# One sum and one reciprocal for a pair of heads, queries and keys in token order, and shorter preparations, in an attention and expert kernel

## The chip, the cores and the metric

The kernel runs on one core of a Trainium2 chip. The core has a matrix engine (TensorE, PE in the profile, with its weight loads shown as PEld), a vector engine (VectorE, DVE), an activation engine (ScalarE, ACT), GpSimd (POOL) and SyncE (SP), which issues nearly all DMAs here. Each engine works through its own queue of instructions in order and waits on semaphores of the others. The metric is the time of one execution in microseconds (us) on the device; the times shown are medians of several executions.

## The reference

Three layers follow each other, on 4 sequences of 576 tokens with width 512 (8 heads of 64):

```python
scores = scale * np.matmul(q, k.transpose(0, 1, 3, 2))
cum = np.cumsum(np.maximum(s, 0.0), axis=-1)
bias = -(cum[:, :, :, None] - cum[:, :, None, :])
scores = np.where(causal, -1000000000.0, scores + np.minimum(bias, 0.0))
attn = np.exp(scores - np.max(scores, axis=-1, keepdims=True))
attn = attn / (np.sum(attn, axis=-1, keepdims=True) + 1e-09)
x = np.matmul(attn, v)                      # attention, heads side by side
h = gelu(x @ w_in); u, v = halves of h      # gated layer
x = x + (u * (w_sg @ layernorm(v) + b_sg)) @ w_out
e = argmax of x @ w_gate, or the token before's choice if sigmoid(x @ w_local) >= 0.5
out = p[e] * (relu(x @ w1[e]) @ w2[e])      # one of 8 experts per token
```

## The kernel before

The attention of all 32 heads runs first, in pairs of heads, mixed with the gated layer of the sequences that are complete; the experts come last. The program is written in Python generators that interleave the stages, and a scheduler then orders the instructions of each engine by its own estimate of when each is ready. A change of one instruction can therefore move others on every engine.

Values are kept as a high part of reduced precision (fp32r) and a low part that is the rest, so that three products stand for one fp32 product.

**Queries and keys.** `prep_load(p)` fetches q and k of a pair of heads into the tiles `nq` and `nk`: 96 partitions, each with 6 neighbouring tokens of both heads (`"h (p r) d -> p r h d"`, one DMA per tile). `prep_T(p, c)` handles half `c`: three transposes on TensorE (L344) put 96 tokens each side by side into a PSUM bank; ACT writes the high part into the tile `qk` (L353 for q, L356 for k), DVE the low part (L354, L357). Since partition p held the tokens 6p to 6p+5, a transpose r gives every sixth token, and the four copies write (and DVE reads) every sixth element of the row: `x.rearrange("p (t r) -> p r t", r=6)`.

**The first four pairs** (sequence 0) are row-tiled: the two heads of a pair lie on partitions 0 to 63 and 64 to 127, and `emit_R(p, i)` computes 128 queries of both. The later pairs go head by head through `emit_S`. For each, DVE adds the causal mask and takes the row minimum (L411), `soft` then has ACT compute the exponential and the row sum (L417), POOL add 1e-9 (L418), DVE take the reciprocal (L419) and POOL scale the rows (L420); L502 transposes the result, DVE and ACT copy it into `et` (L508, L506 for heads 0 to 7), and L541 multiplies it with v. The last 64 queries of both heads are done together (`emit_tail`, L841).

**The sums of s.** `emit_first` makes the running sums for the heads of sequence 0 (eight broadcast DMAs, clamp L223, scan L224, and on to `cumr` at L233), which the first row minimum needs through one matmul. `emit_cum` makes them for all 32 heads, 32 rows on as many partitions: clamp (L239), scan (L241), five subtractions of the value at the start of each block of 128 queries (L246), two copies of the high part (L247), two subtractions for the low part (L248) and two DMAs to a table `cum_d` in memory, out of which later heads fetch their rows. It stands behind the row minimum that was written last when it is reached, in pair 2.

**Constants.** `emit_consts2` builds small tables for the routing to experts: POOL makes them, and some thirteen short DVE instructions convert them (L309 to L330). They have no order with respect to the rest.

The weights of the gated layer come in between as 8-byte numbers and are converted by L723 (ACT), L724 and L727 (DVE), L728 (POOL), L729 (ACT) and L730 (DVE).

## Time and profile before

| | |
|---|---|
| time, median of 3 runs | 843.71 us (842.79 to 845.37) |
| the profiled execution's own time | 844.22 us |
| its span | 842.4 us |
| granted TensorE clock, mean over the span | 0.978 |
| busy: TensorE, weight loads, DVE, ACT, POOL | 792.2, 678.2, 532.1, 449.9, 349.1 us |
| DMA: moved, mean rate | 133.33 MB, 158 GB/s |

The profile is of one execution. Busy times are shares of the span in which the engine had an instruction at work; TensorE's matmuls overlap, and their ends are modelled. The rows further on come from views in order of time (start, duration, engine, line, operation, tiles, and in brackets how long the engine stood idle before and what ended this), from groups of like instructions (busy time, mean of one in ns, idle time before), and from tables of stretches.

### The profile page before, as it was taken

Reading aid. Unit: us, or ns where it says so; the run is one execution under the profiler, and the core shown is the slowest. Engines: PE = TensorE matmul, PEld = TensorE weight load, DVE = VectorE, ACT = ScalarE, POOL = GpSimd, SP = SyncE. Lnnn points to the kernel's source line nnn. Section 1 sums busy time; section 2 is a strip of 40 time slices with the busy share of each in tenths; the row PEclk is TensorE's granted clock in tenths of the full one; section 3 lists DMA queues with packets and bytes.
Section 4 is the critical chain, followed back from the end, with each engine's and each line's share of the span. In section 5 each row is a group of like instructions: output and inputs, shape, how many; then the busy total and the mean of one; then the engine's idle time right before and its main releaser. Section 6 shows DMA issues by size and latency. Waiting matters only on the chain. (4 is left out here: it accounts for less than half of the span.)

```text
span 842.4 us, 14677 instructions
## 1 busy us (share of the span) xinstructions
PE 792.2 (94%) x4828; PEld 678.2 (80%) x4828; DVE 532.1 (63%) x1489; ACT 449.9 (53%) x1040; POOL 349.1 (41%) x627
## 2 busy tenths in 40 slices
PE   8797998989999999999998999989999999999995
PEld 4564687779879889878788788778989989899894
DVE  7777577876768788867786476774555444353420
ACT  5676577766637786527784245134454344443510
POOL 5785556576434387614586001052022222313101
PEclk9699999999999999999999999999999999999998
DMA  8565699794488587587450763144564544535300
GB/s 186 137 184 142 153 229 306 192 237 99 93 192 231 153 214 174 130 238 201 92 179 18 255 220 123 51 139 142 178 211 122 176 127 146 186 126 184 125 5 35
DMA packets 117735, 133.33 MB, mean 158 GB/s; under 512 B 69184, under 2 KB 82624, under 8 KB 117656
## 3 DMA queue, kind: packets, MB, share of 16 engines
q1 hardware_dynamic: 113816, 122.87, 53.6%
q0 software_dynamic: 3840, 9.48, 3.0%
q8 instruction: 40, 0.66, 0.3%
q14 instruction: 39, 0.32, 0.1%
HBM read 91.07 MB, written 23.13 MB: 136 GB/s over the span
## 5 line engine op out<-in xcount | busy, mean ns | idle before, releaser
L1211 DVE TENSOR_TENSOR wp<-wraw,wp 128x1024 fp32r<-128x1024 f32 x63 | 76.6, 1223 | 96.6 <-ACT wp L1210 96.0
L841 PE MATMUL ps<-wp,hT 128*128 128x512 f32 x528 | 123.0, 392 | 0.0
L1267 POOL DMA_INDIRECT out_dram<-y,ids x24 | 34.9, 1454 | 204.6 <-ACT y L1266 157.0
L841 PE MATMUL ps<-xT,wp 128*128 128x384 f32 x672 | 119.1, 336 | 0.0
L841 PEld LDWEIGHTS ps<-xT,wp 128*128 128x128 f32 x672 | 117.3, 188 | 0.7
L841 PEld LDWEIGHTS ps<-wp,hT 128*128 128x128 f32 x528 | 98.6, 188 | 21.1
L1210 ACT CAST wp<-wraw 128x1024 fp32r<-128x1024 f32 x64 | 66.5, 1050 | 65.3 <-DMA wraw<-in_moe_w_dram 58.6
L417 ACT ACTIVATE E<-E,negm 128x128 f32<-128x128 f32 (+4 forms) x136 | 79.1, 582 | 35.5 <-DVE negm L411 30.5
L420 POOL TENSOR_SCALAR E<-E,lsum 128x128 f32<-128x128 f32 (+4 forms) x136 | 79.6, 588 | 38.1 <-DVE lsum L419 28.4
L541 PE MATMUL ps<-et,vv 128*128 128x320 f32 (+9 forms) x476 | 82.7, 314 | 9.9 <-DVE et L508 5.7
L418 POOL TENSOR_SCALAR lsum<-lsum 128x1 f32<-128x1 f32 x144 | 34.5, 240 | 124.7 <-ACT E L417 111.2
L541 PEld LDWEIGHTS ps<-et,vv 128*128 128x128 f32 (+1 forms) x476 | 65.1, 171 | 25.1 <-ACT wsg L247 5.4
L502 PE MATMUL ps<-ident,E 128*128 128x128 f32 (+1 forms) x452 | 69.2, 266 | 8.9 <-POOL E L420 5.5
L411 DVE CUSTOM_DVE_ANT_0 E<-ps,zmask 128x128 f32<-128x128 f32 (+4 forms) x136 | 63.5, 474 | 17.8 <-PE ps L841 15.4
L841 PE MATMUL ps<-wsg,vg 128*128 128x288 f32 x448 | 68.3, 304 | 2.0 <-DVE g L850 1.0
L510 ACT CAST et<-ps 128x384 fp32r<-128x384 f32 (+3 forms) x120 | 50.6, 431 | 33.4 <-PE ps L502 31.4
L841 PEld LDWEIGHTS ps<-wsg,vg 128*128 128x128 f32 x448 | 62.3, 192 | 3.3 <-DVE g L850 1.2
L502 PEld LDWEIGHTS ps<-ident,E 128*128 128x128 f32 (+1 forms) x452 | 48.0, 142 | 20.6 <-POOL E L420 6.9
L511 DVE TENSOR_TENSOR et<-ps,et 128x384 fp32r<-128x384 f32 (+3 forms) x120 | 56.8, 483 | 7.2 <-ACT et L510 6.8
L841 PE MATMUL ps<-xh,w 128*128 128x288 f32 x256 | 57.6, 303 | 0.6 <-DVE negm L411 0.5
L1255 DVE SCALAR_TENSOR_TENSOR hT<-ps,hT 128x384 fp32r<-128x384 f32 x56 | 30.3, 553 | 40.4 <-ACT hT L1254 40.4
L841 PE MATMUL ps<-w,vg 128*128 128x512 f32 (+1 forms) x216 | 54.5, 396 | 0.0
(305 smaller groups left out, 1624.7 us busy)
## 6 DMA issues: line engine op xcount, KB each, us to landing
wraw<-in_moe_w_dram SPq DMA_DIRECT2D x64, 512.0 KB
qk<-qk SPq DMA_DIRECT2D x24, 432.0 KB
w<-wv_d SPq DMA_DIRECT2D x16, 512.0 KB
w<-wo_d SPq DMA_DIRECT2D x16, 512.0 KB
qk<-qk SPq DMA_DIRECT2D x24, 288.0 KB
w<-wu_d SPq DMA_DIRECT2D x12, 512.0 KB
nq<-in_q_dram SPq DMA_DIRECT2D x16, 288.0 KB
nk<-in_k_dram SPq DMA_DIRECT2D x16, 288.0 KB
```

Source lines behind the costliest of these rows:

```text
L411: hred[g] = DVE.tensor_tensor_reduce(out=e[:, a:z], in0=pt[:, 0:z - a], in1=zmask[:, m0:m0 + z - a], scale=-1.0, scalar=BIG if hi == 0 els ...
L417: ACT.activation(out=x, in_=x, func=ACTF.Exp, scale=-1.0, bias=nm, accum_out=l)
L418: POOL.tensor_scalar(out=l, in0=l, scalar1=1e-9, scalar2=0.0, op0=ALU.add, op1=ALU.add)
L420: POOL.tensor_scalar(out=x, in0=x, scalar1=l, scalar2=1.0, op0=ALU.mult, op1=ALU.mult)
L502: PE.transpose(pt[:, j * M:(j + 1) * M], e[h, 128 * j:128 * (j + 1)], ident[h, h])
L510: ACT.copy(out=dst[0], in_=src)
L511: DVE.tensor_tensor(out=dst[1], in0=src, in1=f32v(dst[0]), op=ALU.subtract)
L541: PE.matmul(x, lhsT=l, rhs=rhs if g >= F4 else f32v(rhs), start=(j == 0 and n_ == 0), stop=(j == js[-1] and n_ == len(ms) - 1),)
L841: ms = [PE.matmul(pt, lhsT=l, rhs=r, start=(first_ and x == 0), stop=(last_ and x == n - 1)) for x, (l, r) in enumerate(pairs)]
L1210: c = ACT.copy(out=w[:, 0, :], in_=r)
L1211: a = (POOL if (e, j) == (0, KD) else DVE).tensor_tensor(out=w[:, 1, :], in0=r, in1=f32v(w[:, 0, :]), op=ALU.subtract)
L1267: POOL.indirect_dma_start(out=of[:, :], out_offset=bass.IndirectOffsetOnAxis(ap=idx, axis=0), in_=y, in_offset=None, bounds_check=NT - 1, ...
```

## The change

It consists of five parts.

1. In `soft`, the two heads of a row-tiled pair keep their row sums in two columns of one tile. One addition and one reciprocal serve both columns, after both exponentials.
2. `prep_load` fetches the 576 tokens in two halves of 288, each with 3 neighbouring tokens to a partition: two DMAs per tile with pieces of half the length.
3. `prep_T` places the three transposes of a half so that their columns interleave in the PSUM bank (each writes every third element); the bank then holds 288 tokens in order, and ACT and DVE read and write rows without a step.
4. `emit_cum` handles only the 24 heads of sequences 1 to 3, with one row for each head and block on 120 partitions: five DMAs bring the same rows five times, one clamp and one scan run over all, three short instructions pick the value at each block's start, and one subtraction, one copy, one subtraction and one DMA follow.
5. All DVE instructions of `emit_consts2` are ordered behind the first row minimum of head 1.

```diff
     def emit_cum():
-        R = 128 // NH
-        s_sb = T(mp, [128, S], F32, "u2", bufs=5)[0:NH]
-        dma(s_sb, s.rearrange("b h s -> (b h) s"))
-        behind(DVE.tensor_scalar_max(out=s_sb, in0=s_sb, scalar1=0.0), hred[max(hred)].ins.name)
-        cum = s_sb
-        DVE.tensor_tensor_scan(out=cum, data0=one[0:NH], data1=s_sb, initial=0.0, op0=ALU.mult, op1=ALU.add)
-        for P, i0, z0 in ((128, 0, 6), (NH, R, 8)):
-            tmp = T(mp, [128, S], F32, "u2", bufs=5)
-            ch = wsg[0:P, z0:z0 + 2, :]
-            for a in range(P // NH):
-                DVE.tensor_scalar(out=tmp[NH * a:NH * a + NH], in0=cum, scalar1=cum[:, 128 * (i0 + a):128 * (i0 + a) + 1], scalar2=None, op0=ALU.subtract)
-            ACT.copy(out=ch[:, 0, :], in_=tmp[0:P])
-            DVE.tensor_tensor(out=ch[:, 1, :], in0=tmp[0:P], in1=f32v(ch[:, 0, :]), op=ALU.subtract)
-            dma(cum_d[:, NH * i0:NH * i0 + P, :].rearrange("z p s -> p z s"), ch)
+        n = NH - H
+        P = NQ * n
+        rows, cum = [T(mp, [128, S], F32, "u2", bufs=5)[0:P] for _ in range(2)]
+        src = s.rearrange("b h s -> (b h) s")[H:NH]
+        for i in range(NQ):
+            dma(rows[n * i:n * i + n], src)
+        behind(DVE.tensor_scalar_max(out=rows, in0=rows, scalar1=0.0), hred[max(hred)].ins.name)
+        DVE.tensor_tensor_scan(out=cum, data0=one[0:P], data1=rows, initial=0.0, op0=ALU.mult, op1=ALU.add)
+        m = T(mp, [128, NQ], F32, "m5")[0:P]
+        ref = T(mp, [128, 1], F32, "mr")[0:P]
+        DVE.tensor_reduce(out=m, in_=ident[0:P, 0:P].rearrange("p (i c) -> p i c", c=n), axis=AX.X, op=ALU.add)
+        DVE.tensor_tensor(out=m, in0=cum.rearrange("p (i c) -> p i c", c=64)[:, 0::2, 0], in1=m, op=ALU.mult)
+        DVE.tensor_reduce(out=ref, in_=m, axis=AX.X, op=ALU.add)
+        DVE.tensor_scalar(out=rows, in0=cum, scalar1=ref, scalar2=None, op0=ALU.subtract)
+        ch = wsg[0:P, 6:8, :]
+        ACT.copy(out=ch[:, 0, :], in_=rows)
+        DVE.tensor_tensor(out=ch[:, 1, :], in0=rows, in1=f32v(ch[:, 0, :]), op=ALU.subtract)
+        dma(cum_d.rearrange("z p s -> p z s"), ch)
...
         for src, nm in ((q, "nq"), (k, "nk")):
             t = T(ap_, [96, 6, 2, D], F32, nm)
-            dma(t, src[b, h0:h0 + 2].rearrange("h (p r) d -> p r h d", p=96))
+            for a in range(2):
+                dma(t[:, 3 * a:3 * a + 3], src[b, h0:h0 + 2, HS * a:HS * a + HS].rearrange("h (p r) d -> p r h d", p=96))
...
     def emit_consts2():
+        def late_(x):
+            behind(x, hred[1].ins.name)
...
-        DVE.tensor_copy(out=w8d, in_=it[:, 0:8])
+        late_(DVE.tensor_copy(out=w8d, in_=it[:, 0:8]))
...
             for r in range(3):
-                PE.transpose(pt[:, 96 * r:96 * r + 96], n[:, 3 * c + r].rearrange("p h d -> p (h d)"), ident[0:96, 0:96])
-
-            def v6(x):
-                return x.rearrange("p (t r) -> p r t", r=6)[:, 3 * c:3 * c + 3, :]
-
-            src = pt[:, 0:HS].rearrange("p (r t) -> p r t", r=3)
-            hi = v6(t[:, a, :])
-            lo = v6(t[:, 2 + a, :])
+                PE.transpose(
+                    pt[:, 0:HS].rearrange("p (t r) -> p r t", r=3)[:, r], n[:, 3 * c + r].rearrange("p h d -> p (h d)"), ident[0:96, 0:96]
+                )
+            src = pt[:, 0:HS]
+            hi, lo = [t[:, z, HS * c:HS * c + HS] for z in (a, 2 + a)]
...
-    def soft(x, nm, l):
-        ACT.activation(out=x, in_=x, func=ACTF.Exp, scale=-1.0, bias=nm, accum_out=l)
+    def soft(xs, nms, l):
+        for z, (x, nm) in enumerate(zip(xs, nms)):
+            ACT.activation(out=x, in_=x, func=ACTF.Exp, scale=-1.0, bias=nm, accum_out=l[:, z:z + 1])
         POOL.tensor_scalar(out=l, in0=l, scalar1=1e-9, scalar2=0.0, op0=ALU.add, op1=ALU.add)
         DVE.reciprocal(out=l, in_=l)
-        POOL.tensor_scalar(out=x, in0=x, scalar1=l, scalar2=1.0, op0=ALU.mult, op1=ALU.mult)
+        for z, x in enumerate(xs):
+            POOL.tensor_scalar(out=x, in0=x, scalar1=l[:, z:z + 1], scalar2=1.0, op0=ALU.mult, op1=ALU.mult)
...
-        for r in range(2):
-            soft_of(2 * p + r, i, e[r], nm[r])
+        soft_of(2 * p, i, e, nm)
```

The lines of `prep_T` and `row_min` shift by one: L353 to L357 and L411 of before are L352 to L356 and L410 of after.

The order of instructions moves on all engines. On DVE at the start, before (`u` holds the running sums, `ga` the tables that POOL made, `E` the scores and `negm` their minimum):

```order
L357 TENSOR_TENSOR qk_25_97<-ps,qk_25_97 128x3x96
L320 TENSOR_SCALAR first_84<-s_12_83 128x5
L312 CAST io_8_79<-ga_268 128x128
L223 TENSOR_SCALAR u_39_159<-u_39_159 128x576
L354 SCALAR_TENSOR_TENSOR qk_25_97<-ps,qk_25_97 128x3x96
L313 CAST ioc_80<-ga_268 128x144
L357 TENSOR_TENSOR qk_25_97<-ps,qk_25_97 128x3x96
L316 TENSOR_SCALAR ga_268<-ga_268 128x20
L321 TENSOR_SCALAR ltri_86<-io_8_79,pidx_81 128x128
L224 SCALAR_TENSOR_TENSOR u_40_160<-u_38_148,u_39_159 128x576
```

and after:

```order
L353 SCALAR_TENSOR_TENSOR qk_25_97<-ps,qk_25_97 128x288
L356 TENSOR_TENSOR qk_25_97<-ps,qk_25_97 128x288
L353 SCALAR_TENSOR_TENSOR qk_25_97<-ps,qk_25_97 128x288
L356 TENSOR_TENSOR qk_25_97<-ps,qk_25_97 128x288
L223 TENSOR_SCALAR u_39_161<-u_39_161 128x576
L224 SCALAR_TENSOR_TENSOR u_40_162<-u_38_150,u_39_161 128x576
L226 TENSOR_TENSOR cs_193<-u_40_162,e_44_174 128x5
```

All four low parts of the first pair now precede the clamp L223, and the scan L224 follows it at once; the constants stand behind the first two row minima.

On ACT around the sixth weight tile (`vg`, converted by L723), before:

```order
L729 CAST w_99_541<-vg_542 128x512
L723 ACTIVATE g_116_680<-vg_678 128x512
L417 ACTIVATE E_102_578,lsum_484<-E_102_578,negm_580 128x384
L353 ACTIVATE qk_25_97<-ps 128x3x96
L356 CAST qk_25_97<-ps 128x3x96
L553 COPY xf_457<-ps 64x320
```

and after:

```order
L729 CAST w_101_537<-vg_538 128x512
L352 ACTIVATE qk_25_97<-ps 128x288
L355 CAST qk_25_97<-ps 128x288
L417 ACTIVATE E_104_574,lsum_590<-E_104_574,negm_576 128x384
L723 ACTIVATE g_120_676<-vg_674 128x512
L553 COPY xf_457<-ps 64x320
```

L723 has moved behind the two `qk` copies and the exponential.

On DVE around `emit_cum`, before:

```order
L730 TENSOR_TENSOR vg_831<-vg_831 128x512
L411 ISA E_148_946,negm_948<-ps,zmask_73 128x512
L411 ISA negm_948 128x1
L246 TENSOR_SCALAR u_143_894<-u_142_890 32x576 x3
L419 RECIPROCAL lsum_781<-lsum_781 128x1
L246 TENSOR_SCALAR u_143_894<-u_142_890 32x576
L246 TENSOR_SCALAR u_144_902<-u_142_890 32x576
L411 ISA ga_947,negm_949<-ps,zmask_73 128x512
L411 ISA negm_949 128x1
L508 COPY et_425<-ps 128x5x64
L508 COPY et_425<-ps 128x128
```

and after:

```order
L410 ISA E_154_940,negm_942<-ps,zmask_73 128x512
L410 ISA negm_942 128x1
L730 TENSOR_TENSOR vg_823<-vg_823 128x512
L247 TENSOR_TENSOR m_149_890<-u_148_882,m_149_890 120x5
L410 ISA ga_941,negm_943<-ps,zmask_73 128x512
L410 ISA negm_943 128x1
L419 RECIPROCAL lsum_874<-lsum_874 128x2
L508 COPY et_425<-ps 128x5x64
L508 COPY et_425<-ps 128x128
```

The five subtractions of 576 columns no longer stand ahead of the copies L508; one product of 5 columns does.

## Rows read from the trace of the kernel before

**Rows 1.** The page, busy time of each engine.
```profile
PE 792.2 (94%) x4828; PEld 678.2 (80%) x4828; DVE 532.1 (63%) x1489; ACT 449.9 (53%) x1040; POOL 349.1 (41%) x627
```

**Rows 2.** Stretches: length, busy PE, PEld, DVE, ACT, POOL, clock, DMA share, GB/s.
```profile
8.00:37.00 29.00, 23.13 (x126) 14.59 (x124) 27.90 (x85) 18.82 (x49) 19.64 (x40) 0.77 0.74 166
72.00:76.00 4.00, 3.94 (x12) 1.94 (x12) 2.46 (x10) 1.52 (x5) 3.10 (x5) 0.66 0.49 174
76.00:450.00 374.00, 355.64 (x2451) 308.09 (x2452) 282.87 (x916) 250.51 (x670) 214.45 (x449) 0.99 0.70 180
100.00:160.00 60.00, 56.95 (x397) 48.95 (x396) 43.54 (x128) 42.99 (x119) 32.60 (x67) 0.97 0.95 256
```

**Rows 3.** DVE in order of time, 8 to 16 us: start, duration, engine, line.
```profile
7.95 0.67 DVE L357 TENSOR_TENSOR qk<-ps,qk 128x288 fp32r<-128x288 f32 x1 [0.65 <-ACT qk L356]
...
8.74 0.45 DVE L223 TENSOR_SCALAR u<-u 128x576 f32<-128x576 f32 x1
9.11 0.67 DVE L354 SCALAR_TENSOR_TENSOR qk<-ps,qk 128x288 fp32r<-128x288 f32 x1
...
9.82 0.67 DVE L357 TENSOR_TENSOR qk<-ps,qk 128x288 fp32r<-128x288 f32 x1
...
10.63 1.35 DVE L224 TENSOR_TENSOR_SCAN u<-u,u 128x576 f32<-128x576 f32 x1
...
15.58 0.34 DVE L411 CUSTOM_DVE_ANT_0 E<-ps,zmask 128x128 f32<-128x128 f32 x1
```

**Rows 4.** SP's queue in order of time, the first loads.
```profile
0.73 0.76 SPq L78 DMA_DIRECT2D nq<-in_q_dram  x1
...
2.31 4.43 SPq L200 DMA_DIRECT2D u<-in_s_dram  x8
```

**Rows 5.** Groups by line and shape: count, busy us, mean ns, idle before.
```profile
L356 ACT CAST qk<-ps 128x288 fp32r<-128x288 f32 x32 | 24.3, 758 | 0.9 <-PE ps L344 0.9
...
L354 DVE SCALAR_TENSOR_TENSOR qk<-ps,qk 128x288 fp32r<-128x288 f32 x32 | 22.6, 707 | 6.6 <-ACT qk L353 6.3
...
L357 DVE TENSOR_TENSOR qk<-ps,qk 128x288 fp32r<-128x288 f32 x32 | 22.2, 694 | 0.7 <-ACT qk L356 0.7
...
L850 DVE SCALAR_TENSOR_TENSOR u<-ga,ps 128x288 f32<-128x288 f32 x32 | 14.2, 444 | 1.6 <-ACT ga L849 1.4
...
L511 DVE TENSOR_TENSOR et<-ps,et 128x320 fp32r<-128x320 f32 x24 | 11.6, 483 | 3.7 <-ACT et L510 3.4
...
L510 ACT CAST et<-ps 128x320 fp32r<-128x320 f32 x24 | 10.2, 425 | 10.9 <-PE ps L502 9.5 <-PE ps L541 1.1
```

**Rows 6.** Two lines from 8 to 37 us: count, least, median, most ns.
```profile
L354 DVE SCALAR_TENSOR_TENSOR qk<-ps,qk x4: 659/668/684, 9.1 to 32.1; 128x288 fp32r<-128x288 f32 x4
...
L419 DVE RECIPROCAL lsum<-lsum x13: 139/151/215, 17.2 to 34.4; 128x1 f32<-128x1 f32 x13
```

**Rows 7.** ACT and TensorE in order of time near 41 us.
```profile
40.35 0.66 ACT L723 ACTIVATE g<-vg 128x512 int32<-128x512 uint32 x1 [3.97 <-DMA vg<-in_moe_w_in_dram]
...
42.95 0.96 PE L466 MATMUL ps<-qk 64*128 64x512 f32 x3 [1.14 <-DVE qk L354]
```

**Rows 8.** DVE and TensorE in order of time, near 70 and at 90 us.
```profile
67.72 1.60 DVE L246 TENSOR_SCALAR u<-u 32x576 f32<-32x576 f32 x3
...
69.54 1.27 DVE L246 TENSOR_SCALAR u<-u 32x576 f32<-32x576 f32 x2
...
71.96 3.61 PE L541 MATMUL ps<-et,vv 128*64 128x320 f32 x10 [5.19 <-DVE et L508]
...
90.22 2.27 PE L541 MATMUL ps<-et,vv 128*64 128x320 f32 x10 [0.54 <-DVE et L508]
```

**Rows 9.** The page's DMA queues: packets, MB, share of 16 engines.
```profile
q1 hardware_dynamic: 113816, 122.87, 53.6%
```

**Rows 10.** TensorE in order of time, transposes of q and k.
```profile
77.73 0.41 PE L344 MATMUL ps<-ident,nq 96*128 96x96 f32 x3
77.98 0.41 PE L344 MATMUL ps<-ident,nk 96*128 96x96 f32 x3
```

More of the change, by code (lines that the diff above doesn't have):

```diff
@@ L188 @@
     vt = T(ap_, [128, 4, D], F32, "vt")
-    cum_d = dram.tile([2, NQ * NH, S], F32, name="cum_d")
+    cum_d = dram.tile([2, NQ * (NH - H), S], F32, name="cum_d")
     def slot(z, dt=F32R):
@@ L197, in emit_first @@
         rows, cum, t1 = [T(mp, [128, S], F32, "u2", bufs=5) for _ in range(3)]
-        for g in range(GD):
-            z = cblk(g)
-            (POOL if g in SW else SP).dma_start(out=rows[z:z + 16], in_=s[0, g:g + 1, :].to_broadcast([16, S]))
+        for g in range(H):
+            z = 64 * (g % 2) + 16 * (g // 2)
+            SP.dma_start(out=rows[z:z + 16], in_=s[0, g:g + 1, :].to_broadcast([16, S]))
         e = [T(mp, [128, NQ], F32, f"e{z}") for z in range(3)]
@@ L308, in emit_consts2 @@
         POOL.iota(it[:, 320:320 + B * NQ], pattern=[[-S, B], [-128, NQ]], base=FREE, channel_multiplier=-1)
-        DVE.tensor_copy(out=w8d, in_=it[:, 0:8])
-        DVE.tensor_copy(out=s8, in_=it[:, 8:8 + NQ])
-        DVE.tensor_copy(out=pidx, in_=it[:, 16:17])
-        DVE.tensor_copy(out=io128, in_=it[:, 32:160])
-        DVE.tensor_copy(out=ioc, in_=it[:, 160:160 + NC])
+        late_(DVE.tensor_copy(out=w8d, in_=it[:, 0:8]))
+        late_(DVE.tensor_copy(out=s8, in_=it[:, 8:8 + NQ]))
+        late_(DVE.tensor_copy(out=pidx, in_=it[:, 16:17]))
+        late_(DVE.tensor_copy(out=io128, in_=it[:, 32:160]))
+        late_(DVE.tensor_copy(out=ioc, in_=it[:, 160:160 + NC]))
         tk = it[:, 320:320 + B * NQ]
         hl = it[:, 384:384 + B * NQ]
-        DVE.tensor_scalar(out=hl, in0=tk, scalar1=6, scalar2=None, op0=ALU.logical_shift_right)
-        DVE.tensor_copy(out=wtok[:, 0], in_=hl)
-        DVE.tensor_scalar(out=tk, in0=tk, scalar1=63, scalar2=None, op0=ALU.bitwise_and)
-        DVE.tensor_copy(out=wtok[:, 1], in_=tk)
-        DVE.tensor_scalar(out=first, in0=s8, scalar1=9.0, scalar2=None, op0=ALU.is_equal)
-        DVE.tensor_scalar(out=ltri, in0=io128, scalar1=pidx, scalar2=None, op0=ALU.is_gt)
+        late_(DVE.tensor_scalar(out=hl, in0=tk, scalar1=6, scalar2=None, op0=ALU.logical_shift_right))
+        late_(DVE.tensor_copy(out=wtok[:, 0], in_=hl))
+        late_(DVE.tensor_scalar(out=tk, in0=tk, scalar1=63, scalar2=None, op0=ALU.bitwise_and))
+        late_(DVE.tensor_copy(out=wtok[:, 1], in_=tk))
+        late_(DVE.tensor_scalar(out=first, in0=s8, scalar1=9.0, scalar2=None, op0=ALU.is_equal))
+        late_(DVE.tensor_scalar(out=ltri, in0=io128, scalar1=pidx, scalar2=None, op0=ALU.is_gt))
         POOL.memset(onesb, 1.0)
@@ L327, in emit_consts2 @@
         n = E + 1
-        DVE.tensor_tensor(out=ii, in0=ident[0:2 * n, 0:n], in1=ident[0:2 * n, n:2 * n], op=ALU.add)
+        late_(DVE.tensor_tensor(out=ii, in0=ident[0:2 * n, 0:n], in1=ident[0:2 * n, n:2 * n], op=ALU.add))
         dma_after(1, gcol, g_ln.rearrange("(k p) -> p k", p=128))
-        DVE.tensor_scalar(out=gcol, in0=gcol, scalar1=0.5, scalar2=None, op0=ALU.mult)
+        late_(DVE.tensor_scalar(out=gcol, in0=gcol, scalar1=0.5, scalar2=None, op0=ALU.mult))
     Tst = {}
@@ L366, in prep_asm @@
         rs = slice(64 * r, 64 * r + 64)
-        dma(dst[64:KX, 3, :], cum_rows[g])
+        dma(dst[64:KX, 3, :], cum_rows[g - H])
         if buf[g] not in selected:
@@ L377, in prep_cum @@
         for r in range(2):
-            dma(czp[64 * r:64 * r + 2, :], cum_rows[2 * p + r, NQ - 1::NQ, :])
+            dma(czp[64 * r:64 * r + 2, :], cum_rows[2 * p + r - H, NQ - 1::NQ, :])
     VG = 4
@@ L401, in prep_V @@
             POOL.tensor_tensor(out=lo, in0=x, in1=f32v(hi), op=ALU.subtract)
-    Et, lsum, hred = {}, {}, {}
+    Et, hred = {}, {}
     def spans(i):
@@ L425, in etile, with soft_of @@
         return T(ap_, [128, 128 * (i + 1)], F32, f"E{i}", bufs=2 if i < 2 else 1)
-    def soft_of(g, i, e, nm):
-        if i == 0:
-            lsum[g] = T(ap_, [128, 4], F32, "lsum", bufs=4)
-        Et[g, i] = e
-        soft(e[:, 0:128 * i + 128], nm[:, 0:1], lsum[g][:, i:i + 1])
+    def soft_of(g, i, es, nms):
+        l = T(ap_, [128, 2], F32, "lsum", bufs=8)
+        for z, e in enumerate(es):
+            Et[g + z, i] = e
+        soft([e[:, 0:128 * i + 128] for e in es], [nm[:, 0:1] for nm in nms], l[:, 0:len(es)])
     def negm():
@@ L478, in emit_S @@
         row_min(e, pt, nm, 0, i, 0, n, g)
-        soft_of(g, i, e, nm)
+        soft_of(g, i, [e], [nm])
     ets = {}
```

8 lines of the change are left out of this document (2 added, 6 removed).

## The prediction, made before the changed kernel ran

> **What bounds the kernel now.** I read the page's busy times first, then the stages, then the rows in order of time at each place where TensorE waits. TensorE is busy 792.2 us of the span of 842.4 [rows 1]; the reader is to see that at most 50 us can be won by filling its gaps, and that its own work is not touched by the change (the same matmuls, the same number of transposes). So I ask stage by stage which engine the gaps belong to. From 8 to 37 us VectorE (DVE) is busy 27.90 of 29.00 us: this stretch ends when DVE has done its list, not when TensorE has. TensorE's longest gap, 5.19 us before 72 us, also ends on DVE, on a copy that stands late in its queue [rows 8]. From 76 to 450 us it is the other way round: TensorE 355.64 of 374.00, DVE 282.87 [rows 2]. After 450 us the changed code no longer runs, and that part of the program keeps its order. What the change saves on DVE, ScalarE (ACT) and GpSimd (POOL) therefore counts fully in the first 72 us and very little later.
>
> **Part 1, the start (8 to 37 us).** The chain there is: score sums land, clamp (L223), scan (L224), three more steps, `cumr`, first row minimum. Now L223 starts at 8.74, the scan only at 10.63, because two of the `qk` low parts and four constants lie between them, and the first minimum runs at 15.58 [rows 3]. Three things change.
> a) q and k are fetched by four DMAs in place of two, ahead of the eight that bring the sums. One issue takes 0.76 on SP; the eight take 4.43 and follow at once [rows 4]. Two more issues delay the sums by about 1.4 us if their landing is what L223 waits for (it starts as soon as DVE gets to it, so the landing was at 8.74 or before; I take 8.74). L223 then starts at about 10.1, which is later than DVE's solid work begins now (7.95): 2.15 us given away.
> b) DVE meets the sums with less in hand. The three `qk` steps now at 7.95, 9.11 and 9.82 are done by then; each takes 0.67 us, of which 0.08 lies under the next start (L223 ends at 9.19, L354 starts at 9.11): 3 by 0.6, 1.8 us back. The constants only change place, behind the first minimum; the few that now ran before 7.95 cost some 0.4 us inside the full stretch. Net of a) and b): 2.15 - 1.8 + 0.4 = +0.75.
> c) The steps get cheaper. L354 and L357 take 707 and 694 ns with a write (and a read of the high part) of every sixth element. Contiguous steps of this kind from PSUM take 444 (L850, same 288 columns), and L511, which writes fp32r as these do, 483 at 320 columns [rows 5]. I take 450: 0.22 us less than the 668 of this stretch; six of them for the second and third pair: 1.3 us. Of the 13 reciprocals here 12 belong to pairs, six go at 0.15: 0.9 us [rows 6].
> Part 1 in all: +0.75 - 1.3 - 0.9 = -1.45 us. Bounds: -2.8 if the sums were there well before 8.74; +0.9 if the `qk` steps stay as dear and the sums gate.
>
> A rule bears on c). The rows show 694 ns for 288 elements with a step of 24 bytes against 444 without. The Trainium skill (SBUF — State Buffer, "Door 1: The DMA port swizzle") says that SBUF lines hold 16 bytes, and an access that goes on to a new line each time pays for it; by it all 64 DVE and 64 ACT steps get cheaper, as I assume. The same paragraph says that PSUM lines hold 8 bytes and that any PSUM pattern that is not contiguous slows matmuls much. That speaks against this change, which moves the step from SBUF into the transposes' PSUM writes; it is the third rival below.
>
> **Part 2, ACT's queue at 36 to 43 us.** Now ACT stands still for 3.97 us at L723, which waits for a weight tile, and the exponential of the next pair and L353/L356 are queued behind it; so L354 comes late and TensorE waits 1.14 us for it at 42.95 [rows 7]. In the new order L353, L356 and the exponential stand ahead of that L723. Their inputs come out of TensorE before 40 us in the order of its queue, so the wait goes: -1.1 us. What is late next is L723 itself, and its results feed only a store of weights. Bounds: 0 to -1.1.
>
> **Part 3, the sums of the other heads (64 to 72 us).** TensorE waits 5.19 us for L508, a copy that stands in DVE's queue behind the five subtractions of `emit_cum`. Their two rows last 1.60 and 1.27: 2.8 us [rows 8]. In the new order one 5-column product stands there, and the reciprocal as before. The copy comes 2.7 us earlier, and so does TensorE: -2.7. The clamp and the scan run over 120 partitions in place of 32, at no cost: L223 does 128 partitions in 0.45. The five DMAs that bring the rows are issued long before (some 20 us into the span), in a queue that then waits for buffers anyway. What stays late after this is the copy behind the second minimum, about 2.5 us of gap. Bounds: 0 (another wait ends there last) to -3.3 (ACT's second copy, a subtraction and a second DMA go too).
> After the gap the granted clock is 0.66 for 4 us [rows 2], and ten matmuls take 3.61 us that take 2.27 later [rows 8]. A shorter gap may leave the clock up: 0 to -1.3; I take -0.6.
>
> **Part 4, 76 to 450 us.** TensorE's gaps here are 374.00 - 355.64 = 18.4 us. DVE's saving is 48 `qk` steps by 0.25 = 12 us of 283, 4%; ACT's is more (L356 takes 758 where L510 takes 425 at 320 columns [rows 5]), POOL's is a few adds. Most gaps end on short chains of two or three instructions that are not shortened; I let the gaps shrink by the same 4%: -0.7. Bounds 0 to -3.
>
> **Part 5, the loads.** Per pair 384 pieces become 768 of half the size. At the mean of all pieces (53.6% of 16 times 842.4 us over 113816 pieces, 63 ns [rows 9]) the 384 more cost (384 by 63 ns, over 16) 1.5 us of all 16 DMA engines, if halves cost as much as wholes, and nothing if cost goes by bytes. DMA is busy 0.95 from 100 to 160 us [rows 2], where two pairs load. I take +0.5; bounds 0 to +3. The merged adds and reciprocals also make the first head of a pair wait for the second's exponential; its transposes come several steps later in TensorE's order, so I put this at 0, and at one step of ACT, under 0.8 (L356's 758 ns), if that cover is gone in the first pair.
>
> **Sum.** -1.45 - 1.1 - 2.7 - 0.6 - 0.7 + 0.5 = -6.05, from the profiled execution's 844.22 us (span 842.4, and 1.8 around it): 838.2. That execution lay 0.5 above the median of 843.71, so the median should come out at 837.7; I say 838.
>
> **Rivals.**
> 1. *The `qk` copies get no cheaper* (their price is not the step's but the bank's or fp32r's). For: no row shows ACT or DVE writing this very tile contiguously. Against: L850 and L511 read the same bank and write fp32 and fp32r at 444 to 483. Then 1c keeps only 0.9, and parts 2 and 4 shrink to -0.9 and 0: +0.75 - 0.9 - 0.9 - 2.7 - 0.6 + 0.5 = -2.85, 841.
> 2. *The gain is swallowed between 100 and 160 us*: DMA is nearly full there, so the weights and the assembled heads arrive when the DMA engines have moved the bytes, however early TensorE asks. For: 0.95 busy, twice the pieces. Against: TensorE idles only 3 of these 60 us, and none of its waits names a DMA. Then about -0.5: 843.
> 3. *Slower: the transposes pay for the step of 12 bytes in PSUM.* Three now follow each other every 0.25 us [rows 10], 83 ns each. No row of this kernel shows a matmul that writes PSUM with a step, so the price lies between nothing and a doubling: 0 to 83 ns by 192 = 16 us. Of these, 144 fall after 76 us, where TensorE is the bound: 12 us, against the 6 won: 850. It decides from 40 ns a transpose on (6 us over 144). For: it is the one new thing on the engine that bounds. Against: weight loads keep pace with these transposes (PEld has one for each), so part of a dearer write would hide behind them. The rule on PSUM lines above would put the kernel at this time.
>
> **How the numbers follow.** The forecast (832 to 841) has 0.55; rival 1 has 0.08, rival 2 0.14, rival 3 0.18 (with anything else that makes it slower, such as the late sums at the start); a larger gain than 12 us 0.05. The bounds of the parts, if all came together, add to -11.5 and +3.9 us (832.7 and 848.1); the range takes them in, and reaches over rivals 1 and 2 and into the cheaper half of rival 3: 832 to 849, with about 0.05 left out below and 0.12 above. A difference of 0.3% (2.5 us) is the least that can be told from none here. Faster by more: forecast, larger gain and half of rival 1, 0.64. Within: rival 2, the other half of rival 1 and a little of rival 3, 0.16. Slower: 0.20.
>
> **What would show it.** L353 to L357 at 400 to 460 ns in place of 694 to 758; the transposes still 83 ns apart (a wider step is rival 3); the first minimum near 15 us; no 4 us stop of ACT before the pair's exponential near 40; TensorE's gap before the P·V matmuls near 70 at about 2.5 us; the rest of the span shifted as a whole, by 5 to 6 us from 76 us to the end. The prediction is wrong if the lead at 76 us is not there, or is there and gone by 200.

## The result, and the profile after

The changed kernel runs at 833.84 us, median of four executions (831.45 to 841.32), against 844.54 for the kernel before, measured beside it: ratio 0.987, 95% interval 0.9836 to 0.9905, some 10.7 us faster. The forecast of 838 had the side right and the size too small (6.05 us), and the time lies inside the range. The profiled execution was the slowest of the four (841.32, span 839.4), so the same kernel was profiled once more, in a later run (e5_again below): that execution took 832.50 us, span 830.6; the median of its six is 835.10 against 846.72 before, ratio 0.9878 [0.9855, 0.99]. I call these the first and the second profile.

The page of the first profile, busy times, beside [rows 1]:

```profile
PE 793.6 (95%) x4828; PEld 680.7 (81%) x4828; DVE 511.5 (61%) x1471; ACT 436.9 (52%) x1039; POOL 336.0 (40%) x611
```

DVE lost 20.6 us of work, ACT 13.0, POOL 13.1; TensorE's did not fall. Now the stretches of [rows 2] in the first profile (length; busy PE, PEld, DVE, ACT, POOL; granted clock; DMA share; GB/s):

```profile
8.00:37.00 29.00, 23.58 (x123) 14.56 (x123) 24.02 (x80) 17.43 (x48) 17.71 (x32) 0.81 0.71 175
72.00:76.00 4.00, 4.00 (x38) 3.27 (x38) 2.09 (x8) 3.06 (x10) 2.37 (x3) 1.00 0.87 228
76.00:450.00 374.00, 357.02 (x2477) 311.54 (x2478) 272.11 (x918) 241.13 (x669) 215.30 (x446) 0.99 0.69 179
100.00:160.00 60.00, 57.22 (x412) 50.14 (x412) 42.32 (x132) 43.69 (x123) 32.65 (x66) 1.00 0.95 258
```

In the first stretch DVE is no longer full (24.02 of 29.00, 27.90 before). In the third it lost 10.8 us of 283, and TensorE got busier by 1.4, although its work did not grow (being ahead, it runs 26 more of its matmuls inside this fixed window).

The four copies of `qk` and the transposes of the first profile, groups by line and shape (count, busy us, mean ns, idle before), beside [rows 5, 10]:

```profile
L346 PE MATMUL ps<-ident,nq 96*128 96x96 f32 x96 | 14.4, 261 | 0.0
...
L353 DVE SCALAR_TENSOR_TENSOR qk<-ps,qk 128x288 fp32r<-128x288 f32 x32 | 14.4, 450 | 4.4 <-ACT qk L352 4.3
...
L356 DVE TENSOR_TENSOR qk<-ps,qk 128x288 fp32r<-128x288 f32 x32 | 14.3, 447 | 1.2 <-ACT qk L355 1.2
...
L346 PE MATMUL ps<-ident,nk 96*128 96x96 f32 x96 | 13.9, 256 | 0.7 <-DMA nk<-in_k_dram 0.4 <-DVE qk L353 0.3
...
L352 ACT ACTIVATE qk<-ps 128x288 fp32r<-128x288 f32 x32 | 13.1, 409 | 12.2 <-PE ps L346 10.1 <-issue 1.9
...
L355 ACT CAST qk<-ps 128x288 fp32r<-128x288 f32 x32 | 12.8, 399 | 1.9 <-PE ps L346 1.8
```

DVE's two took 707 and 694 before, ACT's 758 for k; the transposes are what they were, and groups of three still start every 0.25 us (at 73.23, 73.48 and 73.73 in the first profile). The start on DVE, in order of time, beside [rows 3]:

```profile
9.33 0.46 DVE L223 TENSOR_SCALAR u<-u 128x576 f32<-128x576 f32 x1 [0.51 <-DMA u<-in_s_dram]
9.89 1.36 DVE L224 TENSOR_TENSOR_SCAN u<-u,u 128x576 f32<-128x576 f32 x1
...
15.50 0.29 DVE L410 CUSTOM_DVE_ANT_0 E<-ps,zmask 128x128 f32<-128x128 f32 x1 [1.03 <-PE ps L467]
```

The scan comes 0.74 us sooner, yet the first minimum is only 0.08 earlier (0.54 in the second profile): it now waits 1.03 for TensorE. At the end of this stretch TensorE is late, not early. Its transposes of q there, before and in the first profile:

```profile
36.60 0.73 PE L344 MATMUL ps<-ident,nq 96*128 96x96 f32 x3
```
```profile
37.30 0.74 PE L346 MATMUL ps<-ident,nq 96*128 96x96 f32 x3
```

ACT near 41 us, and TensorE's gap near 67 us, beside [rows 7, 8]:

```profile
38.85 0.62 ACT L417 ACTIVATE E<-E,negm 128x384 f32<-128x384 f32 x1
...
40.76 0.67 ACT L723 ACTIVATE g<-vg 128x512 int32<-128x512 uint32 x1 [1.20 <-DMA vg<-in_moe_w_in_dram]
```
```profile
67.15 3.92 PE L541 MATMUL ps<-et,vv 128*64 128x320 f32 x10 [2.87 <-DVE et L508]
```

The exponential stands ahead of the weight's wait, and the gap of 5.19 is 2.87. TensorE's wait of 1.14 for L354 is gone, but the P·V products behind it, which did not wait before, now do (before, then the first profile):

```profile
47.53 2.27 PE L541 MATMUL ps<-et,vv 128*64 128x320 f32 x10
```
```profile
46.04 2.27 PE L541 MATMUL ps<-et,vv 128*64 128x320 f32 x10 [0.78 <-DVE et L508]
```

The granted clock there, before and in the first profile (1.00 is the upper of its two levels, 2.4 GHz, and 0.50 the lower, 1.2 GHz; values between are means over a window that has both):

```profile
42.00:46.00 4.00, 3.06 (x15) 2.70 (x16) 3.91 (x12) 2.14 (x7) 1.95 (x4) 0.75 1.05 166
46.00:50.00 4.00, 3.91 (x18) 2.58 (x17) 3.89 (x14) 3.62 (x9) 3.63 (x7) 0.82 0.07 12
```
```profile
42.00:46.00 4.00, 3.27 (x27) 2.58 (x25) 4.00 (x13) 2.69 (x7) 2.32 (x3) 1.00 0.95 208
46.00:50.00 4.00, 3.64 (x18) 2.13 (x19) 2.37 (x8) 3.11 (x8) 3.77 (x8) 1.00 0.25 94
```

To see where the time went I take the start of a step that occurs once a block in both kernels (ACT's copy `stg<-ps`, 128x512, line L571) and subtract. Negative is ahead of before:

| stage of before, us | first profile | second profile | forecast |
|---|---|---|---|
| 0 to 51.5 | -1.31 | -1.63 | -2.55 (parts 1, 2) |
| 51.5 to 76.6 | -3.19 | -4.50 | -3.3 (part 3) |
| 76.6 to 176.3 | +1.68 | -1.06 | -0.2 (parts 4, 5, both stages) |
| 176.3 to 461.6 | -6.13 | -5.78 | |
| 461.6 to the end | +5.95 | +1.17 | 0 |

The largest term is the stage from 176 to 462 us, where I had expected a fraction of a microsecond. The two profiles of one kernel differ in the third and the last stage. In the first, TensorE waited at 94 us for the v of a pair, which the second does not show:

```profile
PE ps L541 <- DMA vv<-in_v_dram: 2.6, 1, 2.6
```

In the last stage the granted clock fell twice in the first profile (windows of it, columns as above):

```profile
470.00:480.00 10.00, 7.51 (x43) 6.67 (x42) 4.14 (x8) 2.31 (x4) 0.00 (x0) 0.84 0.93 301
480.00:490.00 10.00, 10.00 (x68) 9.80 (x68) 8.39 (x41) 3.86 (x10) 0.00 (x0) 0.82 0.55 176
...
550.00:560.00 10.00, 8.37 (x43) 7.68 (x43) 6.67 (x19) 1.89 (x4) 6.35 (x6) 0.66 0.52 148
```

and once in the second:

```profile
470.00:480.00 10.00, 8.44 (x53) 8.00 (x54) 4.89 (x22) 2.42 (x7) 0.00 (x0) 0.83 0.86 282
```

The kernel before has one such fall too:

```profile
550.00:560.00 10.00, 7.11 (x46) 6.21 (x45) 8.62 (x27) 3.16 (x6) 4.95 (x5) 0.83 0.28 74
```

Near 475 us both profiles wait for expert weights (`w<-wu_d`, 1.3 and 1.5 us), which the kernel before, arriving later, does not. The code of that stage is the same in both kernels.

### The profile page after: what moved, and what is told of

It reads as the page before. It is cut to its first block, busy times and chain, and to the rows that moved or that the text cites. A ratio compares the mean times of both kernels' runs of the same rounds, so it can differ in the third digit from the quotient of the medians.

```text
span 839.4 us, 14673 instructions
## 1 busy us (share of the span) xinstructions
PE 793.6 (95%) x4828; PEld 680.7 (81%) x4828; DVE 511.5 (61%) x1471; ACT 436.9 (52%) x1039; POOL 336.0 (40%) x611
## 3 DMA queue, kind: packets, MB, share of 16 engines
q1 hardware_dynamic: 114363, 122.89, 53.2%
## 5 line engine op out<-in xcount | busy, mean ns | idle before, releaser
L1267 POOL DMA_INDIRECT out_dram<-y,ids x24 | 30.0, 1252 | 214.2 <-ACT y L1266 175.9
L541 PE MATMUL ps<-et,vv 128*128 128x320 f32 (+9 forms) x476 | 85.8, 322 | 8.0 <-DVE et L508 4.1
L410 DVE CUSTOM_DVE_ANT_0 E<-ps,zmask 128x128 f32<-128x128 f32 (+4 forms) x136 | 63.5, 471 | 18.6 <-PE ps L841 13.7
L418 POOL TENSOR_SCALAR lsum<-lsum 128x1 f32<-128x1 f32 (+1 forms) x128 | 31.2, 244 | 108.0 <-ACT E L417 95.1
L841 PE MATMUL ps<-xh,w 128*128 128x288 f32 x256 | 60.4, 313 | 3.0 <-DVE wsg L827 1.5
```

Of the source, the lines that this page charges most:

```text
L410: hred[g] = DVE.tensor_tensor_reduce(out=e[:, a:z], in0=pt[:, 0:z - a], in1=zmask[:, m0:m0 + z - a], scale=-1.0, scalar=BIG if hi == 0 els ...
L418: POOL.tensor_scalar(out=l, in0=l, scalar1=1e-9, scalar2=0.0, op0=ALU.add, op1=ALU.add)
L541: PE.matmul(x, lhsT=l, rhs=rhs if g >= F4 else f32v(rhs), start=(j == 0 and n_ == 0), stop=(j == js[-1] and n_ == len(ms) - 1),)
L841: ms = [PE.matmul(pt, lhsT=l, rhs=r, start=(first_ and x == 0), stop=(last_ and x == n - 1)) for x, (l, r) in enumerate(pairs)]
```

## The experiments

**Theory:** the unexpected stage is the price of the `qk` copies: DVE's queue is shorter, and TensorE's many short waits, which end on DVE, shrink with it. **Rivals:** the order of instructions, which every edit reshuffles, made the difference; or one of the other parts did.

### One part at a time

Each is the kernel before with some hunks of the change. e1_token, the loads in halves and the interleaved transposes (parts 2 and 3 of the change):

```diff
-            dma(t, src[b, h0:h0 + 2].rearrange("h (p r) d -> p r h d", p=96))
+            for a in range(2):
+                dma(t[:, 3 * a:3 * a + 3], src[b, h0:h0 + 2, HS * a:HS * a + HS].rearrange("h (p r) d -> p r h d", p=96))
...
-            hi = v6(t[:, a, :])
...
+            hi, lo = [t[:, z, HS * c:HS * c + HS] for z in (a, 2 + a)]
```

> Only the token order of queries and keys (halved loads, interleaved transposes, rows without a step), on the kernel before. Theory 1 (the rows of after: the copies fell from 694 to 758 ns to 399 to 450, and TensorE's gaps from 176 to 462 us shrank by 4.4 us): this part alone gives more than half of the change, 5 to 8 us faster than before (0.991 to 0.994), with most of it won between 170 and 450 us. Rival (the new orders of instructions, not the prices, made the gain): 0 to 2 us faster.

e2_cum, `emit_cum` on 120 rows alone:

```diff
-            for a in range(P // NH):
-                DVE.tensor_scalar(out=tmp[NH * a:NH * a + NH], in0=cum, ...
...
+        DVE.tensor_scalar(out=rows, in0=cum, scalar1=ref, scalar2=None, op0=ALU.subtract)
```

> Only the 120-row sums. Theory 1: the gap of 5.19 us before the P V matmuls near 70 us shrinks to about 2.5 and the lead of 2.7 us stays: 2 to 3.5 us faster (0.996 to 0.998). Rival (the lead is taken back by a later wait, on a DMA or on the clock): within 1 us of before.

e3_soft, the shared addition and reciprocal alone:

```diff
-    def soft(x, nm, l):
+    def soft(xs, nms, l):
```

> Only the shared addition and reciprocal of a row-tiled pair. Theory 1: 16 reciprocals at 0.157 and 16 additions at 0.24 us go, a third of them in stretches where VectorE is full: 0.5 to 1 us faster. Rival (the first head waits for the second's exponential and TensorE's transposes wait with it): 0.5 to 2 us slower.

e4_consts, the constants behind the first row minimum alone:

```diff
-        DVE.tensor_copy(out=w8d, in_=it[:, 0:8])
+        late_(DVE.tensor_copy(out=w8d, in_=it[:, 0:8]))
```

> Only the constants' VectorE steps behind the first row minimum of head 1. Theory 1: the first minimum comes about 1 us earlier, the later ones lose it again: within 0.5 us of before. Rival (the start decides through the softmax chain and the clock): 1 to 2 us to either side.

Measured against before on the same chip (median 847.0 us), ratio and 95% interval: e1_token 0.9916 [0.9887, 0.9946], -7.1 us; e2_cum 0.9899 [0.985, 0.9948], -8.6; e3_soft 0.9971 [0.9938, 1.0003], -2.5; e4_consts 1.0006 [0.9977, 1.0035], +0.5. In size the token order and the constants came as expected, the shared sums cannot be told from nothing, and `emit_cum` gave more than the 2 to 3.5 us foreseen, in a wide interval. The trace of e2_cum has the mechanism to size. DVE from the scan to the second copy that TensorE waits for, in e2_cum:

```profile
62.05 1.34 DVE L243 TENSOR_TENSOR_SCAN u<-u,u 120x576 f32<-120x576 f32 x1
...
65.26 0.66 DVE L506 COPY et<-ps 128x320 f32<-128x320 f32 x2
```

and in the kernel before:

```profile
65.26 1.33 DVE L241 TENSOR_TENSOR_SCAN u<-u,u 32x576 f32<-32x576 f32 x1
...
71.34 0.67 DVE L508 COPY et<-ps 128x320 f32<-128x320 f32 x2
```

From 6.08 to 3.21: 2.87 us, where part 3 said 2.7. The scan over 120 partitions takes what it took over 32. But the four parts add to -17.7 us, the whole gives -10.7, and e2_cum and e3_soft were 3.2 and 3.3 us ahead at 51 us, before `emit_cum` runs. Nor did e1_token win most of its time between 170 and 450 us, as expected: of its lead only 2.25 us arise from 176 to 462 us of before, and e2_cum, whose copies are as dear as before, won 3.0 there. The two stages (columns as in [rows 2]; before has 285.32 and DVE 220.00):

```profile
174.00:457.07 283.07, 271.78 (x1891) 242.83 (x1890) 213.91 (x723) 178.02 (x489) 163.82 (x338) 0.99 0.61 161
```
```profile
173.39:455.70 282.31, 269.88 (x1882) 240.14 (x1882) 219.94 (x712) 182.67 (x486) 162.34 (x335) 0.99 0.62 161
```

So the next question was the order.

### The order of instructions

In the kernel before, the halving of a bias row (`bbc`, L1400, 1.44 us at 25.45) stands ahead of the second pair's row minima (the expectation below calls it the third); in e1_token, e2_cum and the changed kernel it stands behind some of them. e8_bbc_later moves that alone:

```diff
-        DVE.tensor_scalar(out=bbc, in0=bbc, scalar1=0.5, scalar2=None, op0=ALU.mult)
+        behind(DVE.tensor_scalar(out=bbc, in0=bbc, scalar1=0.5, scalar2=None, op0=ALU.mult), hred[max(hred)].ins.name)
```

> The kernel before, with one DVE instruction moved: the halving of the bias row bbc (1.44 us at 25.45 in the profile before) is ordered behind the latest row minimum, by which the scheduler also changes the place of a few steps of the weight conversion near 28 to 35 us. No part of the change is in it. Theory: a part of what three of the single edits gave (leads of 2.3 to 3.3 us at 51 us, before anything they edit can have saved that much) is this: any edit moved that instruction behind the row minima of the third pair, and with them the release of the buffer that the next weight tile waits for, so that ACT's stop of 3.97 us went. Then the row minimum that stood at 26.81 stands near 25.4, ACT's stop at L723 is 2 us or less, TensorE is 1.4 to 3.3 us ahead at 51 us, and the kernel is 1 to 3 us faster. Rival: the lead comes from the edits themselves; then nothing is ahead at 51 us by more than 1 us, and the time stays within 1 us.

Ratio 1.0001 [0.9979, 1.0023]. The minimum moved from 26.81 to 25.41 as expected, but ACT's stop stayed (e8_bbc_later, ACT):

```profile
39.21 0.66 ACT L723 ACTIVATE g<-vg 128x512 int32<-128x512 uint32 x1 [3.81 <-DMA vg<-in_moe_w_in_dram]
```

The kernel was 1.17 us ahead at 51 us, 0.31 at 76, and nothing at the end. This theory falls: that instruction is not what put the single edits ahead, and a lead of a microsecond in the first 51 us is not kept by itself.

The traces show where that lead arises. From TensorE's transposes at 36.60 us before to its P·V products at 47.53, the four single edits gain 2.3 to 3.2 us on the kernel before, and the two profiles of the changed kernel 2.2 and 2.4; e8_bbc_later gains 0.3. It alone keeps ACT's stop (3.81 us; at most 1.2 in the others), and its clock from 42 to 46 us is 0.57, against 1.00 in the others. Even e4_consts, which touches neither the copies nor the weights, has this gain: in the single edits L723 still stands ahead of the exponential, but its weight has landed (it waits 0.99 us at most). So four single gains hold it four times, which is one reason why they add to more than the whole. Later, too, orders move the time: in e3_soft and e8_bbc_later, whose copies are dear as in e2_cum, the stage from 176 us is 287.15 and 287.40 us long, against 282.31 there, as wide a spread as the gain to be explained.

### The whole without a part

e10_no_token is the changed kernel with the old loads, transposes and copies (the hunk of e1_token left out), e11_no_consts the changed kernel without the hunk of e4_consts.

> The changed kernel without part 2 and 3 of the change: queries and keys loaded, transposed and copied as before, all else as changed. Theory of the price: it loses what the token order alone gave, 5 to 9 us (about 839 to 843). Rival: the parts share their gain, since each alone takes away the same waits (ACT's stop near 40 us, some of the short waits on DVE later), and the kernel without this part is 0 to 4 us slower than the changed one (834 to 838).

> The changed kernel without part 5: the constants of the routing keep their old place. By the run with that part alone (ratio 1.0006) it is worth nothing, so this runs at the changed kernel's time within 2 us (833 to 836). Rival: the constants behind the first row minimum cost the full stretch before 37 us some 0.5 to 1.5 us, which the rest of the change hides when it is measured whole; then this is 1 to 3 us faster (831 to 833) and is the better kernel.

e10_no_token: 0.9961 [0.9942, 0.9981], 844.64 us against 847.41, so the token order is worth 0.9961 - 0.9878 = 0.8%, 7.0 us, beside the other parts, as it was alone (7.1). The other three together are worth 3.3 us (1.6 to 4.9); the 8.6 of e2_cum alone, from six executions, does not return there, and its excess over the trace's 2.87 stays unexplained. e11_no_consts: 833.80 us, ratio 0.9833 [0.9803, 0.9863]. Against the 0.9878 of the changed kernel the difference is 0.0045, by the two intervals 0.6 to 7 us; against the first 0.987 it is not clear of noise. So "worth nothing" is not borne out by these times, and whether the kernel is better without this part stays open: in its profile TensorE starts the transposes shown above at 35.05 us in place of 37.30, but at 176 us it is 5.9 us ahead of before, between the 2.8 and 7.2 of the two profiles. As to the rival that the parts share their gain: in the whole times the token order does not, but ACT's stop near 40 us, which that expectation names, is taken away by each of the four alone.

### The price of the copies, in one order

The next five kernels have the changed kernel's instructions on every engine in its order, and one of them is that kernel itself (e5_again). Only access patterns differ.

> The changed kernel unaltered, as the base for the next two. Theory: ratio to the kernel before 0.984 to 0.990, as first measured (8 to 13 us faster), the copies L352 to L356 at 400 to 450 ns, and the gaps of TensorE between 176 and 462 us about 10 us in place of 14.8. Rival: the wait for v near 94 us and the one for expert weights near 477 us, which its first profile showed, come again; then its profile lies near 840 us whenever it is taken, and is no accident of one execution.

e6_sbuf_step: transposes side by side, the copies write SBUF with a step of 12 bytes.

```diff
-                    pt[:, 0:HS].rearrange("p (t r) -> p r t", r=3)[:, r], ...
+                    pt[:, 96 * r:96 * r + 96], ...
...
-            src = pt[:, 0:HS]
-            hi, lo = [t[:, z, HS * c:HS * c + HS] for z in (a, 2 + a)]
+            src = pt[:, 0:HS].rearrange("p (r t) -> p r t", r=3)
+            hi, lo = [t[:, z, HS * c:HS * c + HS].rearrange("p (t r) -> p r t", r=3) for z in (a, 2 + a)]
```

> The changed kernel, with the three transposes side by side in PSUM (no step there), and the four copies of qk reading PSUM in rows and writing SBUF with a step of 12 bytes (24 before the change). Loads, sums, reciprocals and constants stay as changed. Theory: what the token order gave was the copies' price, and that price is the step's on the SBUF side: the copies are back at 600 ns or more, and the kernel is 3 to 7 us slower than the changed one (about 837 to 841 if that runs at 834). Rival 1: 12 bytes are small enough that the copies stay at 400 to 480 ns; then the time is that of the changed kernel within 2 us. Rival 2: the copies are dear again but the time stays, and the token order's gain came from another thing, such as the order of the instructions.

e7_psum_read: the same, with the step on the reading side, in PSUM.

```diff
...
+            src = pt[:, 0:HS].rearrange("p (r t) -> p t r", r=3)
+            hi, lo = [t[:, z, HS * c:HS * c + HS].rearrange("p (t r) -> p t r", r=3) for z in (a, 2 + a)]
```

> The changed kernel, with the three transposes side by side in PSUM, and the copies reading PSUM out of step (every 96th element, three at a time) and writing SBUF rows without one; the second copy also reads the high part in SBUF without a step. Theory: only the step on the SBUF side was dear, so the copies stay at 400 to 480 ns, and the time is that of the changed kernel within 2 us. Rival: a step on either side costs alike: 600 ns or more, and 3 to 7 us slower than the changed kernel.

e9_step24: the changed kernel's transposes, copies at the old step of 24 bytes.

```diff
-            src = pt[:, 0:HS]
-            hi, lo = [t[:, z, HS * c:HS * c + HS] for z in (a, 2 + a)]
+            src = pt[:, 0:HS].rearrange("p (t r) -> p r t", r=6)
+            hi, lo = [t[:, z, HS * c:HS * c + HS].rearrange("p (t r) -> p r t", r=6) for z in (a, 2 + a)]
```

> The changed kernel; only the four copies of qk read PSUM and read and write SBUF with the old step of 24 bytes (six passes over every sixth element in place of one row; the values and places are the same). Loads, transposes and all else stay as changed, TensorE's, POOL's and SP's orders too. Theory of the price: it is the 250 to 300 ns of each copy that shortened TensorE's gaps; then the copies are at 650 to 760 ns and the kernel is 3 to 7 us slower than the changed one (about 837 to 841), with the gaps between 176 and 462 us back near 14 us. Rival, for which the run at 12 bytes speaks: the copies lie beside other work, and the time stays within 2 us of the changed kernel (833 to 836).

e12_act24: the step of 24 bytes for ACT's two copies alone.

```diff
+            hs, ss = [x.rearrange("p (t r) -> p r t", r=6) for x in (hi, src)]
...
-                ACT.mul(out=hi, in_=src, mul=0.125)
+                ACT.mul(out=hs, in_=ss, mul=0.125)
...
-                ACT.copy(out=hi, in_=src)
+                ACT.copy(out=hs, in_=ss)
```

> The changed kernel; only the two ACT copies of qk (high parts) go back to the step of 24 bytes, while DVE's two (low parts) keep rows. The order of instructions on every engine is that of the changed kernel. With both engines at 24 bytes the ratio to before was 0.992 in place of 0.987. Theory: the waits of TensorE that came back there between 176 and 462 us end on DVE, so it is DVE's price that counts; then ACT's copies are at 690 to 760 ns, DVE's at 450, and the ratio is 0.984 to 0.989, as changed. Rival: DVE's copy waits for ACT's high part, so a later ACT copy holds up DVE's queue as a dearer DVE copy does; then the ratio is 0.990 to 0.994, and DVE's idle time before L353 that ends on ACT rises from about 4.5 us to 8 us or more.

| kernel | DVE copies, ns | ACT copies, ns | ratio to before | 95% interval |
|---|---|---|---|---|
| e5_again | 451, 448 | 408, 398 | 0.9878 | 0.9855 to 0.99 |
| e7_psum_read | 451, 447 | 407, 397 | 0.9866 | 0.9831 to 0.9901 |
| e6_sbuf_step | 551, 547 | 560, 560 | 0.9864 | 0.9842 to 0.9886 |
| e12_act24 | 453, 452 | 709, 754 | 0.987 | 0.9844 to 0.9895 |
| e9_step24 | 706, 698 | 702, 751 | 0.992 | 0.9891 to 0.9948 |

The stage from 176 to 462 us of before, from its first to its last such `stg` copy (stretch; length; busy PE, PEld, DVE, ACT, POOL; clock; DMA). Before:

```profile
176.32:461.64 285.32, 270.50 (x1875) 239.60 (x1876) 220.00 (x712) 182.34 (x487) 161.91 (x336) 0.99 0.63 160
```

the changed kernel, second profile:

```profile
169.13:448.67 279.54, 270.10 (x1889) 240.99 (x1888) 211.68 (x719) 177.10 (x490) 163.72 (x338) 0.99 0.63 163
```

e6_sbuf_step:

```profile
168.50:449.04 280.54, 270.73 (x1889) 241.16 (x1888) 214.86 (x719) 180.24 (x490) 163.37 (x338) 0.99 0.63 163
```

e12_act24:

```profile
172.31:452.41 280.10, 269.33 (x1883) 240.23 (x1883) 213.62 (x722) 183.56 (x490) 164.78 (x339) 0.99 0.62 163
```

e9_step24:

```profile
171.22:454.95 283.73, 270.21 (x1884) 239.17 (x1884) 220.59 (x722) 184.09 (x490) 164.94 (x339) 1.00 0.61 161
```

and e10_no_token:

```profile
170.48:457.10 286.62, 273.27 (x1891) 242.86 (x1890) 221.63 (x719) 183.83 (x490) 163.13 (x338) 0.99 0.63 160
```

The reader is to put the column of DVE beside the length. In these rows DVE at 212 to 215 goes with a stage of 280, at 220 to 222 with 284 to 287; ACT at 183.56 goes with 280.10, so ACT's price is not felt while DVE's copies are cheap. (e1_token and e2_cum, in other orders, do not fit: 214 with 283, 220 with 282. So the reading rests on the kernels in one order; the two profiles of the changed kernel differ by 0.35 us in this stage.) With the order as changed but all four copies at the old price (e9_step24), the stage is 4.2 us longer than in the second profile, and the kernel loses 0.5% (0.992 against 0.987, the mean of the four others, 4.2 us; by the intervals some 1.6 to 6.9). So the price is shown to be a cause. Two things in it came out otherwise than the theory said: the first 100 ns of DVE's price cost nothing that the ratio shows (e6_sbuf_step, where I had expected copies of 600 ns or more and 3 to 7 us; its stage is 1.0 us longer), and the last 155 ns together with ACT's did. A run with DVE alone at 24 bytes was not made, so how much ACT adds once DVE is dear stays open.

Among the waits that shrank are short ones that end on DVE. TensorE's waits in this stage that the profile puts down to one such step, a product of two columns in the gated layer's normalization that stands in DVE's queue among the copies (total us, times, longest): before,

```profile
PE ps L502 <- DVE mv L900: 1.6, 2, 0.8
```

second profile,

```profile
PE ps L502 <- DVE mv L900: 0.9, 2, 0.4
```

e9_step24:

```profile
PE ps L502 <- DVE mv L900: 1.5, 2, 0.8
```

Added over all lines, TensorE's named waits on DVE in these stretches are 12.5 us before, 7.5 in the second profile, 7.7 in e6_sbuf_step, 9.2 in e12_act24, 10.6 in e9_step24 and 9.0 in e10_no_token. They follow the length of the stage only roughly: e10_no_token has the longest stage and less of them than e12_act24. That the dear copies delay what stands behind them fits these sums; no run follows a single chain from a copy to a wait. What the price does not explain of the token order's 7.0 us is e9_step24 against e10_no_token, 0.992 against 0.9961: 3.5 us (0.6 to 6.4). The two differ in loads, transposes and order; which of these it is, no run separates. In the stage it is 2.9 us (283.73 and 286.62).

## Why the prediction was right, and where it was too small

**Part 1 (start): wrong, also in sign.** The copies' price (450 taken) measured 450 and 447. L223 now waits for the sums until 9.33, 0.59 us later than it ran before, where I took 1.4. But of the 3.9 us that DVE no longer works between 8 and 37 us nothing arrives at 37: TensorE's transposes there come 0.70 and 0.60 us later than before, where I took -1.45. The premise that the stretch ends when DVE has done its list held only until DVE was relieved; the first minimum now waits for TensorE, and TensorE for POOL's scaled rows (2.81 us before 29.94, 2.43 before). Which part makes these transposes late is not settled: they are late in e1_token (37.47) and e4_consts (38.26), and early in the changed kernel without either of the two (34.50 in e10_no_token, 35.05 in e11_no_consts).

**Part 2 (ACT's queue): right, and too small.** The order is as forecast, L723 waits 1.20 behind the exponential, and TensorE's wait of 1.14 is gone; 0.78 of it returns as a wait for L508 at 46.04. What I left out is the clock: before, it was 0.75 and 0.82 from 42 to 50 us, behind that wait, and now it stays at 1.00. From the transposes at 36.60 to the P·V products at 47.53 the changed kernel gains 2.2 us (2.4 in the second profile), where I took 1.1. That parts 1 and 2, given 2.55 together, still brought 1.3 to 1.6 is luck: the gain left out of one covers the loss left out of the other.

**Part 3 (the other heads' sums).** Right at the gap: 2.87 of 2.7 on DVE; the gap is 2.87 where I said about 2.5, and TensorE gains 2.3 and 2.1 us over it. That the stage gave -3.2 and -4.5 of -3.3 is in part chance: the rest was won between 51 and 65 us, where I had taken nothing, and the 0.6 taken for the clock is not there. After the gap the clock still falls (4 us at 0.66 before, 0.68 from 68 to 72 us now, and back at 1.00 from 72 to 76), its mean from 64 to 76 us is 0.86 before and in both profiles, and the ten matmuls behind the gap, with 3.92 us, got no faster. The lead that was to be seen at 76 us was there (4.5 and 6.1 us), and 2.8 and 7.2 of it were left at 176.

**Part 4 (76 to 450 us): the term that was mis-sized.** I took -0.7, by letting TensorE's gaps shrink in proportion to DVE's saving, "Most gaps end on short chains of two or three instructions that are not shortened". The stage from 176 us on alone gave -5.8 to -6.1, below even my bound of -3. The saving itself was right (8.3 us of DVE in this stage, 12 forecast for all of 76 to 450). What failed is the proportion: gaps fell from 14.8 to 9.4 us, 36%, for 4% of DVE's time. As I read it, a short chain begins when DVE reaches it, and the dear copies stood in the queue before it. For each microsecond of DVE the stage gave 0.7 (5.8 of 8.3, before to the second profile, token loads and order included), 0.5 (4.2 of 8.9, e9_step24 to the second profile, the price alone) or 0.3 (1.0 of 3.2, e6_sbuf_step to the second profile). So some 4 of the 5.8 us are the price; the rest is loads or order, and orders alone move this stage by as much (shown with e8_bbc_later).

**Part 5 (the loads).** DMA's time did not rise (53.2% of the span for 114363 packets, 53.6% for 113816 [rows 9]); that is the net of more `qk` pieces and fewer for the sums, so what halves cost is not shown apart. A wait for v at 94 us (first profile only) and for expert weights near 475 us (both) are new.

**Rivals.** Copies no cheaper: fallen. (Its terms as written add to -3.85 and 840, not to -2.85 and 841; nothing else rests on this.) Swallowed by DMA between 100 and 160 us: not there (57.22 busy of 60), but a like loss stands beside it in the first profile: of the 8.8 us between the two profiles 2.7 lie from 76 to 176 us, with the wait for v, and 4.8 in the last stage, at the low clocks shown above. Slower transposes: fallen. They take 261 ns with a PSUM step of 12 bytes and 261 and 263 without (e6_sbuf_step, e7_psum_read, `nq`), and start 0.25 us apart by threes either way. The Trainium skill (SBUF — State Buffer, "Door 1: The DMA port swizzle") has any non-contiguous PSUM pattern slow matmuls; the trace does not agree for these, and the measurement decides.

## What to carry to other kernels

When TensorE waits many times for short steps of another engine, look at what stands ahead of those steps in that engine's queue: here, with the order held fixed, a third to a half of a saving there came through in the stage, with that engine three quarters busy, where proportion to its busy time gave less than a tenth. To tell a price from an order, change only the access pattern, so that every engine's order stays as it is; the single parts, each with its own order, here all won 2 to 3 us at one and the same place. And a stage in which nothing changed can still take back time (1.2 and 6.0 us in the two profiles), where an earlier arrival meets a transfer that has not landed and the clock falls.
